# A gated dilated convolution: the first lines of x loaded in pieces of 112 and 15 partitions, and the zero halo written after the transpose

## The chip, the core and the metric

The kernel runs on one core of a Trainium2 chip. The metric is the device time of one execution in microseconds, the median of several. The profile is of one execution; its span runs from the first to the last instruction of the core and is about 2 us shorter than the time.

## The reference

```python
B, T, D, K = (2, 16000, 144, 15)          # x: (B, T, D), w: (K, D, 2D), w_o: (D, D), all bfloat16
dil = 2
pad = (K - 1) * dil                       # 28
xp = jnp.pad(x, ((0, 0), (pad, 0), (0, 0)))
h = jnp.einsum('btc,cd->btd', xp[:, pad:pad + T, :], w[0])
for i in range(1, K):
    off = pad - i * dil
    h = h + jnp.einsum('btc,cd->btd', xp[:, off:off + T, :], w[i])
f = h[..., :D].copy()
g = h[..., D:].copy()
z = jnp.tanh(f) * _sigmoid(g)
return z @ w_o
```

A causal convolution along time with 15 taps, two steps apart; tanh of one half of the channels times the sigmoid of the other; then a projection. In front of each of the two batches stand 28 lines of zeros, the halo.

## The kernel before

The 32000 lines of x are cut into 128 segments of L = 250 lines, one for each partition; partitions 0 to 63 are batch 0 and 64 to 127 batch 1 (SEG = 64). A partition needs the H = 28 lines ahead of its segment too. For all partitions but two these are the last lines of the segment before. For partitions 0 and 64, where a batch begins, they are zero.

The tile Xp holds the first 38 lines of each partition (28 of halo, 2 odd ones up to E0 = 30, and one group of 8, an "octet"). It is loaded in four pieces along time: lines 0 to 14, 14 to 22, 22 to 30 and 30 to 38. The text calls them x0, x1, x2 and x3. Weights come in four pieces of 3 or 4 taps, w3 first. Xr is the tile for the chunks of 16 lines that follow.

```python
LOADS = [("x", 0), ("w", 3), ("w", 2), ("x", 1), ("w", 1), ("x", 2), ("x", 3), ("r", 0), ("w", 0)]
pro_pieces = [(0, 14), (14, 22), (22, E0), (E0, EP)]
...
# x0, x1, x2: two loads of 63 partitions each (1..63 and 65..127)
for i, p0 in enumerate((0, SEG)):
    g.add("sp", ld_x(flat(Xp[p0 + 1:p0 + SEG, e0:e1, :]), p0 + 1, p0 + SEG, e0, e1), w=[("Xp", pi, i)], ...)
...
# partitions 0 and 64: the two real lines by a load, the 28 zero lines by four memsets on VectorE
for p0 in (0, SEG):
    g.add("act", ld_x(flat(Xp[p0:p0 + 1, H:E0, :]), p0, p0 + 1, H, E0), w=[("Xp", 2, 2 + p0)], ...)
for zi, (e0, e1) in enumerate(((0, 14), (14, H))):
    for p0 in (0, SEG):
        g.add("dve", lambda v, ...: v.memset(flat(Xp[p0:p0 + 1, e0:e1, :]), 0.0), w=[("XpZ", zi, p0)], dur=1.1)
```

Channels 0 to 127 of each line are transposed on TensorE, so that channels lie on partitions; the result is copied from PSUM into XA, one octet at a time, by VectorE for the first and ScalarE for the others. Channels 128 to 143 are copied by ScalarE into XBc, from where four lines at a time are transposed later into XB. A warm-up of 40 matmuls stands ahead of the first transposes in TensorE's order.

```python
warm(40)
...
for pi in range(4):
    for o in range(-4, 1):                   # octets -4 .. 0, those that begin in this piece
        ...
        g.add("pe", fns, r=xp_keys[pi] + ["ID"], alloc=[bk], ...)            # transposes (L575)
        eng = "dve" if o == -4 else "act"
        g.add(eng, ev, r=[bk], w=[("XA", aslot(o))], frees=[bk], ...)        # PSUM -> XA (L584)
    compact_pro(pi)                          # channels 128.. -> XBc, on ScalarE (L544, L562)
hk = ["XBc_h%d" % i for i in range(4)]
hk5 = hk + ["XBc_h4"]
for o, tiles, bb in ((-1, range(E0 - 4, E0), 7), (0, range(E0, E0 + 8), 6)):
    ...                                      # transposes of XBc (L594), copied to XB by ScalarE (L598)
```

The first ten output lines of each segment are computed directly, 15 taps each, from XA and the weights ("direct" matmuls); the scheduler uses them to fill TensorE's time until the main part runs. The main part forms differences of lines and sums of weights on VectorE (V, DU, DD, GX, GU, GV, GD; WC, WS, WT, WD) and needs fewer matmuls for each line. Its lines come from Xr, copied by ScalarE into STA (L637) and transposed by DMA.

Each operation is given to a small list scheduler in the kernel, with the keys that it reads (`r`) and writes (`w`) and an assumed duration; from these the order on each engine and the semaphore waits are worked out. All matmuls of the convolution have one source line, L725, and all main loads of x have L475.

Of the kernel before, what the change touches and what calls it, by code (L numbers as in the profile page):

```python
# [11 lines left out]
NP = 128  # L12
# [315 lines left out]
def _conv_wavenet_kernel(nc, x, w, w_o, out):  # L328
    B, T, D = x.shape
    K = w.shape[0]  # L330
    DIL = 2
    DA = 128
    DB = D - DA
    N2 = 2 * D
    total = B * T
    L = total // NP
    SEG = T // L
    H = DIL * (K - 1)
    assert (B, T, D, K) == (2, 16000, 144, 15) and L * NP == total and T % L == 0
    NT = L  # L340
    KD = NT % 8
    NOCT = NT // 8
    assert KD == 2
    E0 = H + KD
    NE_ALL = L + H
    MB = (NE_ALL + 2) // 4 + 1
# [30 lines left out]
    with contextlib.ExitStack() as st:  # L377
        def sb(name, shape, dt):
            return st.enter_context(nc.sbuf_tensor(name, shape, dt))

        Xp = sb("Xp", [NP, EP, D], BF16)
        Xr = sb("Xr", [NP, NX, XCH, D], BF16)
        XBc = sb("XBc", [NP, 8, MB, DB], BF16)
        STA = sb("STA", [NP, NST, 8, 128], BF16)
        STB = sb("STB", [NP, NST, 12, 128], BF16)
        XA = sb("XA", [NP, NA, 8, 128], BF16)
# [26 lines left out]
        x_t, w_t, wo_t, out_t = x.tensor, w.tensor, w_o.tensor, out.tensor  # L413

        g = _Graph()
# [25 lines left out]
        def aslot(o):  # L441
            return (o + 4) % NA
# [7 lines left out]
        def bslot(o):  # L450
            return (o + 1) % NB

        def oct_of(e):
            return (e - E0) // 8, (e - E0) % 8
# [9 lines left out]
        def win_b(e):  # L464
            c4, m4 = (e + 2) % 4, (e + 2) // 4
            return XBc[:, 4 + c4, MB - 1 - m4:MB - 1 - m4 + 8, :].rearrange("p m c -> p (m c)")
# [5 lines left out]
        def ld_x(tile_ap, p0, p1, e0, e1):  # L472
            def f(e):
                src = bass.AP(x_t, (p0 * L - H + e0) * D, [[L * D, p1 - p0], [1, (e1 - e0) * D]])
                return e.dma_start(tile_ap, src)  # L475
            return f

        def flat(ap):
            return ap.rearrange("p e d -> p (e d)")
# [4 lines left out]
        def ld_w(t0, t1):  # L484
            def f(e):
                src = bass.AP(w_t, t0 * D * N2, [[N2, DA], [D * N2, t1 - t0], [1, N2]])
                return e.dma_start(WA[:, t0:t1, :], src)  # L487
            return f
        wa_pieces = [(0, 4), (4, 8), (8, 12), (12, 15)]
        LOADS = [("x", 0), ("w", 3), ("w", 2), ("x", 1), ("w", 1), ("x", 2), ("x", 3), ("r", 0), ("w", 0)]  # L490
        pro_pieces = [(0, 14), (14, 22), (22, E0), (E0, EP)]
        def load_xchunk(ci):
            a, c = CH[ci]
            s = ci % NX
            return g.add("sp", ld_x(flat(Xr[:, s, 0:c - a, :]), 0, NP, E0 + a, E0 + c), w=[("Xr", s)], dur=0.5, dma="xr", nbytes=NP * (c - a) * D * 2)

        wa_ops = {}
        for what, pi in LOADS:
            if what == "w":
                t0, t1 = wa_pieces[pi]  # L500
                wa_ops[pi] = g.add("sp", ld_w(t0, t1), w=[("WA", pi)], dur=0.42, dma="wa", nbytes=(t1 - t0) * 128 * N2 * 2)
                continue
            if what == "r":
                load_xchunk(pi)
                continue
            e0, e1 = pro_pieces[pi]
            if e0 >= H:
                g.add("sp", ld_x(flat(Xp[:, e0:e1, :]), 0, NP, e0, e1), w=[("Xp", pi, 0), ("Xp", pi, 1)], dur=0.48, dma="xp", nbytes=NP * (e1 - e0) * D * 2)
                continue
            for i, p0 in enumerate((0, SEG)):  # L510
                g.add("sp", ld_x(flat(Xp[p0 + 1:p0 + SEG, e0:e1, :]), p0 + 1, p0 + SEG, e0, e1), w=[("Xp", pi, i)], dur=0.48, dma="xp", nbytes=63 * (e1 - e0) * D * 2)
        for p0 in (0, SEG):
            g.add("act", ld_x(flat(Xp[p0:p0 + 1, H:E0, :]), p0, p0 + 1, H, E0), w=[("Xp", 2, 2 + p0)], dur=0.5, dma="xp", nbytes=576)
        for zi, (e0, e1) in enumerate(((0, 14), (14, H))):
            for p0 in (0, SEG):
                g.add("dve", lambda v, p0=p0, e0=e0, e1=e1: v.memset(flat(Xp[p0:p0 + 1, e0:e1, :]), 0.0), w=[("XpZ", zi, p0)], dur=1.1)
        xpz = [[("XpZ", zi, p0) for p0 in (0, SEG)] for zi in range(2)]
        xp_keys = [[("Xp", 0, 0), ("Xp", 0, 1)] + xpz[0], [("Xp", 1, 0), ("Xp", 1, 1)] + xpz[1],
                   [("Xp", 2, 0), ("Xp", 2, 1), ("Xp", 2, 2), ("Xp", 2, 2 + SEG)] + xpz[1], [("Xp", 3, 0), ("Xp", 3, 1)]]
        wa_op = wa_ops[0]  # L520

        def ld_wb(par):
            n = 8 - par
# [25 lines left out]
        def warm(n):  # L549
            bk = _Bank(BANK_O)  # L550
            g.add("pe", [lambda t: t.matmul(PS[:, BANK_O * 512:BANK_O * 512 + 128], lhsT=ID[:], rhs=ONES[:], start=True, stop=True)] * n,
                  r=["ID", "ONES"], alloc=[bk], frees=[bk], dur=0.07 * n)
# [3 lines left out]
        def compact_pro(pi):  # L556
            e0, e1 = pro_pieces[pi]
            if pi == 0:
                def f2(a):
                    s = Xp[:, 0:2, DA:D]  # L560
                    dst = bass.AP(XBc[:].tensor, 6 * MB * DB + (MB - 1) * DB, [[8 * MB * DB, NP], [MB * DB, 2], [1, DB]])
                    return a.activation(dst, s, ACT.Copy)  # L562
                g.add("act", f2, r=xp_keys[0], w=["XBc_h0"], dur=0.25)
                e0 = 2
            cmp_op("act", Xp[:, e0:e1, DA:D], e0, e1, xp_keys[pi], "XBc_h%d" % (pi + 1), 0.35)
        for pi in range(4):
            e0, e1 = pro_pieces[pi]
            for o in range(-4, 1):
                es = [e for e in range(max(0, E0 + 8 * o), E0 + 8 * o + 8)]
                if not (e0 <= es[0] < e1):  # L570
                    continue
                b = 6 + o % 2
                fns = []
                for e in es:
                    fns.append((lambda e_, b_, i_: (lambda t: t.transpose(PSb[:, b_ * 1024 + 128 * i_:b_ * 1024 + 128 * i_ + 128], Xp[:, e_, 0:DA], ID[:])))(e, b, oct_of(e)[1]))  # L575
                bk = _Bank(b)
                g.add("pe", fns, r=xp_keys[pi] + ["ID"], alloc=[bk], dur=0.06 * len(es))
                i0 = oct_of(es[0])[1]
                eng = "dve" if o == -4 else "act"

                def ev(v, b_=b, i0_=i0, o_=o, eng_=eng):
                    dst = XA[:, aslot(o_), i0_:8, :].rearrange("p a b -> p (a b)")
                    src = PSb[:, b_ * 1024 + 128 * i0_:b_ * 1024 + 1024]
                    return v.activation(dst, src, ACT.Copy) if eng_ == "act" else v.tensor_copy(dst, src)  # L584
                g.add(eng, ev, r=[bk], w=[("XA", aslot(o))], frees=[bk], dur=0.92 if eng == "act" else 0.6)
            compact_pro(pi)
            warm(WARMS)
        hk = ["XBc_h%d" % i for i in range(4)]
        hk5 = hk + ["XBc_h4"]
        for o, tiles, bb in ((-1, range(E0 - 4, E0), 7), (0, range(E0, E0 + 8), 6)):  # L590
            fns = []
            for e in tiles:
                c0 = bb * 1024 + 128 * oct_of(e)[1]
                fns.append(lambda t, e_=e, c=c0: t.transpose(PSb[:, c:c + 128], win_b(e_), ID[:]))  # L594
            bk = _Bank(bb)
            g.add("pe", fns, r=hk5 + ["XBcz", "ID"], alloc=[bk], dur=0.06 * len(fns))
            i0 = oct_of(tiles[0])[1]
            xb_op = g.add("act", lambda v, o=o, i0=i0, bb=bb: v.activation(XB[:, bslot(o), i0:8, :].rearrange("p a b -> p (a b)"), PSb[:, bb * 1024 + 128 * i0:bb * 1024 + 1024], ACT.Copy),  # L598
                  r=[bk], w=[("XB", bslot(o))], frees=[bk], dur=0.5 if o < 0 else 0.92)
# [275 lines left out]
        def octs(u):  # L875
            m, r = units[u]
            return m, r, 2 * m + 1, 2 * m + 2
# [183 lines left out]
        if ("r", 0) not in LOADS:  # L1061
            load_xchunk(0).deps.add(wa_op)
# [75 lines left out]
        def fetch(o):  # L1138
            while nl[0] < len(CH) and CH[nl[0]][0] <= 8 * o:
                load_xchunk(nl[0]).deps.add(wa_op if nl[0] < 2 else xb2)  # L1140
                nl[0] += 1
# [47 lines left out]
        for t in range(-reach, NUN):  # L1189
# [3 lines left out]
            for name, off in pattern_of(t):  # L1193
# [20 lines left out]
                if name[0] == "D":  # L1214
                    done_d[u] = done_d.get(u, 0) + 1
                    m, r, o0, o1 = octs(u)
# [12 lines left out]
        m, r, o0, o1 = octs(NUN - 1)  # L1229
# [53 lines left out]
def bass_standalone__autoregressive_conv_wavenet__speech_kernel(  # L1283
    nc: bass.Bass,
    x: bass.AP,
    w: bass.AP,
    w_o: bass.AP,
    out: bass.AP,
):
    _conv_wavenet_kernel(nc, x, w, w_o, out)  # L1290
# [28 lines left out]
```

## Time and profile before

| what | value | where from |
|---|---|---|
| time | 325.68 us median of 3 (324.48, 325.68, 325.94) | times |
| span of the profiled execution | 322.6 us | page, first line |
| DVE memsets of the halo (L516) | 4, 898 ns each, from 1.11 to 5.50 us | timeline |
| Xp loads of x0, each half | 63 packets of 4032 B | packet records |
| Xp loads of x1 and x2, each half | 63 packets of 2304 B | packet records |
| granted TensorE clock | 1.000 | clock of the core |

How to read it: PE is TensorE, DVE VectorE, ACT ScalarE, POOL GpSimd and SP SyncE, which issues most of the loads. A line of a timeline has the start in us, the duration in us, the engine, the source line, the operation, what is written and read, the number of instructions put together and, in brackets, how long the engine sat idle ahead of it and what ended that. A line of the list of waits has who waited for whom, the total in us, how often, and the longest. In the chain that ended last a line has start, duration and what held the end at that time.

### The profile page before, as it was taken

How to read it: one execution, taken by the hardware profiler on the slowest of the kernel's cores; microseconds unless marked ns; L12 is line 12 of the kernel's file. 1: busy time of each engine (PE TensorE's matmuls, PEld its weight loads, DVE VectorE, ACT ScalarE, POOL GpSimd, SP SyncE). 2: the span in 40 equal slices, each digit the busy share in tenths (PEclk: the TensorE clock that was granted, in tenths of full speed). 3: DMA queues.
4: the chain of work that ended last, by engine and by line, in shares of the span. 5: the costliest groups of instructions: out<-in, count | busy, mean ns of one | idle time of the engine just before them, and what ended most of it. 6: DMA issues, size and time to landing. Idle time of an engine off the chain costs nothing.

```text
span 322.6 us, 6961 instructions
## 1 busy us (share of the span) xinstructions
PE 314.0 (97%) x2670; PEld 243.0 (75%) x2670; DVE 285.8 (89%) x610; ACT 269.4 (83%) x636; POOL 15.4 (5%) x26
## 2 busy tenths in 40 slices
PE   7899999999999999999999999999999999999994
PEld 6677777777777777777777777777777777777673
DVE  6699989899898989989898999989899998884773
ACT  3599689889798988979798897979889797778674
POOL 8005500000000000000000000000000000000000
PEclk9999999999999999999999999999999999999999
DMA  7799995967779297886959589793958477131653
GB/s 180 221 204 147 265 189 124 170 165 163 191 119 259 58 222 144 125 229 89 251 104 231 129 180 172 117 269 63 218 138 176 104 137 175 44 69 71 112 132 91
DMA packets 127780, 50.38 MB, mean 156 GB/s; under 512 B 119095, under 2 KB 121577, under 8 KB 127747
## 3 DMA queue, kind: packets, MB, share of 16 engines
q1 hardware_dynamic: 127231, 49.61, 74.2%
q0 software_dynamic: 512, 0.33, 0.5%
q8 instruction: 21, 0.34, 0.5%
q14 instruction: 12, 0.10, 0.1%
q10 hardware_dynamic: 4, 0.00, 0.0%
HBM read 11.81 MB, written 9.22 MB: 65 GB/s over the span
## 4 chain that ended last, share of the span: by engine, by line
PE 86%; DVE 4%; ACT 4%; DMA 3%; SPq 1%; issue 1%; ACTq 0%
PE PS L725 76%; PE PS L824 9%; DMA Xr<-in_x_dram 3%; SPq L475 1%; ACT STA L637 1%; ACT STB L657 1%; DVE V L677 1%; DVE Xp L1004 1%; DVE DD L677 1%; ACT XB L598 0%; DVE DU L677 0%; SPq L487 0%; PE PS L855 0%; DVE Z L754 0%; PE PS L782 0%
## 5 line engine op out<-in xcount | busy, mean ns | idle before, releaser
L1004 DVE TENSOR_TENSOR Xp<-PS,UX 128x576 f32<-128x576 f32 x90 | 62.8, 750 | 19.6 <-PE PS L725 19.3
L725 PE MATMUL PS<-WB,XB 128*128 128x288 bf16 x260 | 71.8, 286 | 0.1
L1016 DVE TENSOR_TENSOR PS<-PS,Xp 128x576 f32<-128x576 f32 x90 | 68.2, 757 | 2.1 <-ACT OS L832 1.0
L725 PE MATMUL PS<-WA,GD 128*128 128x288 bf16 x360 | 69.9, 286 | 0.0
L746 ACT ACTIVATE TS<-PS 128x288 f16<-128x288 f32 x125 | 51.6, 413 | 11.7 <-PE PS L725 10.7
L832 ACT ACTIVATE OS<-PS 128x432 bf16<-128x432 f32 (+1 forms) x88 | 42.3, 488 | 13.8 <-PE PS L824 12.8
L749 ACT ACTIVATE TS<-PS 128x288 f16<-128x288 f32 x125 | 51.4, 411 | 0.0
L657 ACT ACTIVATE STB<-XBc 128x768 bf16<-128x768 bf16 x60 | 50.7, 853 | 0.1
L883 ACT ACTIVATE PS<-PS 128x288 f32<-128x288 f32 x120 | 46.2, 407 | 3.6 <-PE PS L725 3.3
L952 ACT ACTIVATE UX<-PS 128x576 f32<-128x576 f32 x60 | 39.3, 655 | 10.3 <-PE PS L725 10.1
L725 PE MATMUL PS<-WS,GU 128*128 128x288 bf16 x210 | 44.3, 287 | 0.0
L824 PE MATMUL PS<-WOR,ZT 128*128 128x144 bf16 (+1 forms) x322 | 42.4, 253 | 0.0
L725 PEld LDWEIGHTS PS<-WA,GD 128*128 128x128 bf16 x360 | 34.6, 98 | 9.8 <-DVE PS L1016 0.9
L754 DVE TENSOR_TENSOR Z<-TS 128x288 bf16<-128x288 f16 x125 | 36.7, 299 | 4.6 <-ACT TS L749 4.3
L725 PE MATMUL PS<-WC,XB 128*128 128x288 bf16 x120 | 34.3, 286 | 0.0
L824 PEld LDWEIGHTS PS<-WOR,ZT 128*128 128x128 bf16 x322 | 27.9, 98 | 6.3 <-ACT OS L832 0.5
L725 PE MATMUL PS<-WD,DD 128*128 128x288 bf16 x180 | 31.9, 286 | 0.5 <-ACT PS L883 0.5
L725 PE MATMUL PS<-WA,DD 128*128 128x288 bf16 x180 | 30.6, 286 | 0.0
L725 PE MATMUL PS<-WC,V 128*128 128x288 bf16 x180 | 30.6, 286 | 0.0
L725 PEld LDWEIGHTS PS<-WB,XB 128*128 128x128 bf16 x260 | 25.4, 98 | 6.7 <-ACT XB L598 0.4
L725 PE MATMUL PS<-WT,DU 128*128 128x288 bf16 x120 | 24.5, 286 | 0.1
L677 DVE TENSOR_TENSOR V<-XA 128x1024 bf16<-128x1024 bf16 (+2 forms) x39 | 23.5, 607 | 0.9 <-ACT XA L584 0.9
(80 smaller groups left out, 464.3 us busy)
## 6 DMA issues: line engine op xcount, KB each, us to landing
Xr<-in_x_dram SPq DMA_DIRECT2D x15, 576.0 KB, 4.6
out_dram<-OS SPq DMA_DIRECT2D x30, 288.0 KB, 3.1
WA<-in_w_dram SPq DMA_DIRECT2D x3, 288.0 KB, 7.6
Xp<-in_x_dram SPq DMA_DIRECT2D x4, 141.8 KB
ZT<-Z SPq DMA_TRANSPOSE x32, 3.7
Xp<-in_x_dram SPq DMA_DIRECT2D x2, 248.1 KB
XA<-STA SPq DMA_TRANSPOSE x30, 3.4
XB<-STB SPq DMA_TRANSPOSE x30, 5.0
```

The lines of the kernel that those rows point to most:

```text
L657: return v.activation(STB[:, q, 6 * h:6 * h + 6, :], src, ACT.Copy)
L677: return g.add("dve", lambda v: v.tensor_tensor(dst, a, b, ALU.subtract), r=r, w=wk, dur=t_tt(n), prio=prio, soft=gate[:1])
L725: return lambda t: t.matmul(bank(bk.b), lhsT=lhs(), rhs=rhs(), start=start, stop=True, skip_group_check=True)
L746: return a.activation(TS[:, s, 0, :, :], both(bk, 0, D), ACT.Tanh)
L749: return a.activation(TS[:, s, 1, :, :], both(bk, D, D), ACT.Sigmoid)
L754: return v.tensor_tensor(dst, TS[:, s, 0, :, :], TS[:, s, 1, :, :], ALU.mult)
L824: return t.matmul(PS[:, c0:c0 + n * D], lhsT=ZT[:, zt, blk, :], rhs=WOR[:, wi:wi + n, :].rearrange("p a b -> p (a b)"), start=first, stop= ...
L832: return e.tensor_copy(dst, src) if eng == "dve" else e.activation(dst, src, ACT.Copy)
L883: g.add("act", lambda e: e.activation(bank(bk.b + 1), bank(bk.b), ACT.Copy), w=[bk], dur=t_act(N2), prio=0)
L952: g.add("act", lambda e: e.activation(UX[:, k, u % NU, :, :], both(X, 0, N2), ACT.Copy), r=[X], w=[("UX", k, u % NU)], frees=[X], dur=t_ac ...
L1004: g.add("dve", lambda v, k=k, wi=wi, vb=vb, us=us: v.tensor_tensor(wslot(wi), both(vb, 0, N2), UX[:, k, us, :, :], ALU.add), r=[vb, ("UX", ...
L1016: return v.tensor_tensor(both(d, 0, N2), src, wslot(wi), ALU.add)
```

## The change

Each of the pieces x0, x1 and x2 is loaded for partitions 1 to 112 by one DMA and for partitions 113 to 127 by another, whatever batch they belong to. Partition 64 so gets the last lines of batch 0 in its halo, and partition 0 gets the first lines of x as a filler, by one more DMA of 8064 bytes, so that nothing unset is read. The zeros are set later: in XA, where the two partitions have become two columns of each transposed line, by four memsets on VectorE, and in XBc by two memsets on GpSimd, each on one partition. These two also clear the two real lines in XBc that share the range, and one more GpSimd copy puts them back. The memsets of Xp are dropped. The purpose is a number of partitions that is a multiple of 16 in the large loads, and no clearing ahead of the transposes. The order of loads, the transposes, the copies and the main part are as before.

```diff
+        n16 = ((NP - 1) // 16) * 16
...
-            for i, p0 in enumerate((0, SEG)):
-                g.add("sp", ld_x(flat(Xp[p0 + 1:p0 + SEG, e0:e1, :]), p0 + 1, p0 + SEG, e0, e1), w=[("Xp", pi, i)], dur=0.48, dma="xp", nbytes=63 * (e1 - e0) * D * 2)
-        for p0 in (0, SEG):
-            g.add("act", ld_x(flat(Xp[p0:p0 + 1, H:E0, :]), p0, p0 + 1, H, E0), w=[("Xp", 2, 2 + p0)], dur=0.5, dma="xp", nbytes=576)
-        for zi, (e0, e1) in enumerate(((0, 14), (14, H))):
-            for p0 in (0, SEG):
-                g.add("dve", lambda v, p0=p0, e0=e0, e1=e1: v.memset(flat(Xp[p0:p0 + 1, e0:e1, :]), 0.0), w=[("XpZ", zi, p0)], dur=1.1)
...
+            g.add("sp", ld_x(flat(Xp[1:1 + n16, e0:e1, :]), 1, 1 + n16, e0, e1), w=[("Xp", pi, 0)], dur=0.48, dma="xp", nbytes=n16 * (e1 - e0) * D * 2)
+            g.add("sp", ld_x(flat(Xp[1 + n16:NP, e0:e1, :]), 1 + n16, NP, e0, e1), w=[("Xp", pi, 1)], dur=0.48, dma="xp", nbytes=15 * (e1 - e0) * D * 2)
+        g.add("act", lambda e: e.dma_start(flat(Xp[0:1, 0:H, :]), bass.AP(x_t, 0, [[L * D, 1], [1, H * D]])), w=[("Xp", 0, 2)], dur=0.5, dma="xp", nbytes=8064)
+        g.add("act", lambda e: e.dma_start(flat(Xp[0:1, H:E0, :]), bass.AP(x_t, 0, [[L * D, 1], [1, KD * D]])), w=[("Xp", 2, 2)], dur=0.5, dma="xp", nbytes=576)
...
+        for o in range(-4, 0):
+            i0 = 2 if o == -4 else 0
+            i1 = 6 if o == -1 else 8
+            def zc(v, o_=o, i0_=i0, i1_=i1):
+                dst = XA[:, aslot(o_), i0_:i1_, :].rearrange("p s (b q) -> p s b q", q=SEG)[:, :, :, 0]
+                return v.memset(dst, 0.0)
+            g.add("dve", zc, w=[("XA", aslot(o))], dur=0.08)
...
+        for b in range(B):
+            def zf(p, b_=b):
+                return p.memset(XBc[b_ * SEG:b_ * SEG + 1, 4:8, MB - H // 4 - 1:MB, :], 0.0)
+            g.add("pool", zf, r=hk, w=hk + ["XBcz"], dur=0.35)
...
+        def fix(p):
+            s = Xp[:, H:E0, DA:D]
+            dst = bass.AP(XBc[:].tensor, 6 * MB * DB + (MB - 1 - H // 4) * DB, [[8 * MB * DB, NP], [MB * DB, 2], [1, DB]])
+            return p.tensor_copy(dst, s)
+        g.add("pool", fix, r=xp_keys[2], w=hk, dur=0.3)
```

More of the change, by code (lines that the diff above doesn't have):

```diff
@@ L509, in _conv_wavenet_kernel @@
                 continue
-            for i, p0 in enumerate((0, SEG)):
-                g.add("sp", ld_x(flat(Xp[p0 + 1:p0 + SEG, e0:e1, :]), p0 + 1, p0 + SEG, e0, e1), w=[("Xp", pi, i)], dur=0.48, dma="xp", nbytes=63 * (e1 - e0) * D * 2)
-        for p0 in (0, SEG):
-            g.add("act", ld_x(flat(Xp[p0:p0 + 1, H:E0, :]), p0, p0 + 1, H, E0), w=[("Xp", 2, 2 + p0)], dur=0.5, dma="xp", nbytes=576)
-        for zi, (e0, e1) in enumerate(((0, 14), (14, H))):
-            for p0 in (0, SEG):
-                g.add("dve", lambda v, p0=p0, e0=e0, e1=e1: v.memset(flat(Xp[p0:p0 + 1, e0:e1, :]), 0.0), w=[("XpZ", zi, p0)], dur=1.1)
[L517 to L520, printed above, removed]
+            g.add("sp", ld_x(flat(Xp[1:1 + n16, e0:e1, :]), 1, 1 + n16, e0, e1), w=[("Xp", pi, 0)], dur=0.48, dma="xp", nbytes=n16 * (e1 - e0) * D * 2)
+            g.add("sp", ld_x(flat(Xp[1 + n16:NP, e0:e1, :]), 1 + n16, NP, e0, e1), w=[("Xp", pi, 1)], dur=0.48, dma="xp", nbytes=15 * (e1 - e0) * D * 2)
+        g.add("act", lambda e: e.dma_start(flat(Xp[0:1, 0:H, :]), bass.AP(x_t, 0, [[L * D, 1], [1, H * D]])), w=[("Xp", 0, 2)], dur=0.5, dma="xp", nbytes=8064)
+        g.add("act", lambda e: e.dma_start(flat(Xp[0:1, H:E0, :]), bass.AP(x_t, 0, [[L * D, 1], [1, KD * D]])), w=[("Xp", 2, 2)], dur=0.5, dma="xp", nbytes=576)
+        wa_op = wa_ops[LOADS[-1][1]] if LOADS[-1][0] == "w" else wa_ops[0]
+        xp_keys = [[("Xp", 0, 0), ("Xp", 0, 1), ("Xp", 0, 2)], [("Xp", 1, 0), ("Xp", 1, 1), ("Xp", 0, 2)],
+                   [("Xp", 2, 0), ("Xp", 2, 1), ("Xp", 0, 2), ("Xp", 2, 2)], [("Xp", 3, 0)]]
         def ld_wb(par):
```

## The prediction

> **What bounds the kernel now.** I read the page's busy shares first, then who waits for whom, the chain that ended last, the start of the timeline, and the DMA packets. On the page, TensorE (PE) is busy nearly all the time:
>
> ```profile
> PE 314.0 (97%) x2670; PEld 243.0 (75%) x2670; DVE 285.8 (89%) x610; ACT 269.4 (83%) x636; POOL 15.4 (5%) x26
> ```
>
> The waits of PE over the whole span are five:
>
> ```profile
> PE PS L551 <- POOL ID L529: 1.7, 1, 1.7
> PE PS L575 <- DMA Xp<-in_x_dram: 1.6, 3, 0.8
> PE PS L725 <- ACT PS L883: 0.5, 1, 0.5
> PE PS L782 <- ACT Xr L777: 0.4, 1, 0.4
> PE PS L725 <- DVE XA L584: 0.2, 1, 0.2
> ```
>
> The change touches the second (the transposes wait for the lines of x) and the fifth. The other three are the wait before the warm-up and two in the last 45 us. Where the second falls is seen in PE's own timeline of the stretch 5 to 15 us:
>
> ```profile
> 4.73 1.14 PE L551 MATMUL PS<-ONES,ID 128*128 128x128 bf16 x11
> 6.33 0.95 PE L575 MATMUL PS<-ID,Xp 128*128 128x128 bf16 x14 [0.46 <-DMA Xp<-in_x_dram]
> 7.50 2.19 PE L725 MATMUL PS<-WA,XA 128*128 128x288 bf16 x15 [0.21 <-DVE XA L584]
> 10.05 0.62 PE L575 MATMUL PS<-ID,Xp 128*128 128x128 bf16 x8 [0.37 <-DMA Xp<-in_x_dram]
> 10.51 1.51 PE L725 MATMUL PS<-WA,XA 128*128 128x288 bf16 x11
> 12.84 0.61 PE L575 MATMUL PS<-ID,Xp 128*128 128x128 bf16 x8 [0.82 <-DMA Xp<-in_x_dram]
> 13.28 1.14 PE L725 MATMUL PS<-WA,XA 128*128 128x288 bf16 x8
> 14.26 0.61 PE L575 MATMUL PS<-ID,Xp 128*128 128x128 bf16 x8
> ```
>
> The warm-up ends at 4.73 + 1.14 = 5.87. From there to 12.84 PE waits 0.46 + 0.37 + 0.82 = 1.65 us for Xp. After 12.84 the list above has nothing until the end phase, so time gained before about 13 us can reach the end, if the other engines keep up. Whether they do is read from the chain that ended last, in order of time:
>
> ```profile
> 4.69 1.13 SPq L475
> 5.86 8.97 DMA Xr<-in_x_dram
> 14.85 1.06 ACT STA L637
> 15.91 0.91 ACT XA L584
> ...
> 39.61 5.43 PE PS L725 x42
> ```
>
> It runs through the first main chunk of x (Xr), landed at 14.83, then without a gap over ScalarE (ACT) and VectorE (DVE) to 39.6 us, where PE takes over. So the gain is the smaller of two shifts: what PE saves before 13 us, and how much sooner Xr lands.
>
> The trace's packet records explain the loads. The first 63-line load of Xp, whose rows are 4032-byte packets, ends in nine 4-byte completion packets (3.49 to 3.72 us), Xr in nine late ones (14.09 to 14.31 us). From 4 to 11 us the core moves some 270 GB/s (mean of half-microsecond bins of packet starts); from about 11.5 us, with Xr not yet finished, the bins fall to 130 to 280 GB/s. Packet durations while loaded: 4032 B 156 ns, 2304 B about 120, 4608 B about 182, 576 B (weights) 31.
>
> **What the Trainium skill says.** "DMA: Bandwidth & Descriptors", section "Why a DMA increments its semaphore by 16 and not by 1": a copy runs on the largest number of engines up to 16 that divides the slowest dimension of both sides, the lowest-numbered ones, and each engine used posts one completion. For 63 lines that is 9, for 112 it is 16, for 15 it is 15, and for all 127 lines in one piece it would be 1, which explains two pieces. The nine completions agree for 63; no trace yet shows 112 or 15. The same page's "Rules for kernel authors" says that two loads of disjoint partition halves both spray over all 16 engines; for 63-line halves this trace differs, with nine. "SBUF — State Buffer", section "SBUF: two separate sides", says that DVE and GpSimd (POOL) share a port pair under an exclusive lock; no contention can be seen here before, because POOL is idle from 7.50 us until it issues the WOR loads at 28.15.
>
> **What is removed.** Engines 0 to 8 carry 14 rows of each of the three Xp pieces, engines 9 to 15 none. Up to Xr, one of the nine carries: x0 14 x 0.156 = 2.18, w3 24 x 0.031 = 0.74, w2 32 x 0.031 = 0.99, x1 14 x 0.120 = 1.68, w1 0.99, x2 1.68, x3 8 x 0.120 = 0.96, Xr 8 x 0.182 = 1.46; sum 10.68 us. After the change each carries 7 + 1 rows per piece. It saves 6 x 0.156 = 0.94 us by x0, another 6 x 0.120 = 0.72 by x1, another 0.72 by x2: 2.38 us by Xr. With all 16 busy throughout, the common rate may bind instead. Xp, the three weight pieces and Xr are 1.40 + 0.81 + 0.59 = 2.80 MB; at 270 GB/s that is 10.4 us, from about 2.4 us (the first packets took 0.47 to 0.59 us each) to 12.8, against a last packet at 14.31. So Xr lands 1.5 us sooner by the rate and 2.4 by the rows; I take 1.5, and 1.1 if the rate is a tenth lower.
>
> The Xp pieces were usable at 6.31, 10.03 and 12.77. By the rows they come at about 5.4, 8.4 and 10.4. The four DVE clears of a halo line (898 ns each, 1.11 to 5.50 us) go too; they ended before x0 was usable, with DVE otherwise idle, so they are worth nothing.
>
> **What it means for PE.** x0 at 5.4 is before the warm-up's end at 5.87, so only 0.46 is gained there. The second transposes would be reached at 9.69 - 0.46 = 9.23 and x1 is there at 8.4: 0.37 gained. The third at 12.02 - 0.83 = 11.19, x2 at 10.4: 0.82 gained. Sum 1.65 us.
>
> **What is added.** Four DVE memsets of at most 128x16 elements, each between the copy of a transposed octet into XA and the matmuls on it. The 128x32 uint32 memset of SCR took 85 ns, so 0.09 each, plus a handoff of some 0.05 (DVE's copy ends at 7.44, PE starts at 7.50), plus the rest of a weight sum that DVE may be in (L608, 300 to 450 ns). For the octet that DVE copies itself I count 0.14; for the next, 0.25, as PE's weight loads already wait for it (8.40). For the last two PE should have other matmuls to do. Sum about 0.4 us. Two POOL memsets on one partition of 512 elements: Z's memset took 3930 ns for 4608, so about 0.44 each; with the copy of 128x32 (an estimate of 0.2, from the 117 ns of POOL's memset of that size) 1.1 us after the third piece's copy into XBc. That was done at 13.08 and XBc is first used at 15.14, so it fits. The junk line for partition 0 is 8064 B, two more rows for one engine, about 0.3 us on x0, covered by the warm-up.
>
> Net: 1.65 - 0.4 = 1.25 us on PE, against 1.1 to 2.4 on the chain through Xr. Expected gain about 1.3 us: 325.7 - 1.3 = 324.4 us.
>
> **The rivals.** (a) The clears become the wait: DVE works in order, and a clear queued behind a sum whose weights are not there holds PE. For it: DVE sat 1.60 us before a WC sum for weights at 11.05. Against it: weights also come sooner. It would eat 0.5 to 1 us more: 325.2 to 325.7. (b) The common rate binds harder than 270 GB/s and Xr hardly moves: ACT, gapless from 14.85 to 24, and DVE behind it then keep their times, and PE runs out of early matmuls and waits: 325.4. For it: bins of 165 to 215 GB/s at 5 to 6 and 8.5 us with all engines at work. Against it: bins of 300 to 349 elsewhere. (c) Everything shifts by the full amount, the clears hidden: 1.65 to 2.2 us, 323.5 to 324.0. (d) The kernel orders its instructions by an internal plan; other operations may reorder DVE and ACT work later, by some tenths either way.
>
> **Range and chances.** Mechanism: 0.2 to 2.1 us of gain. The three times before lie 1.46 us apart, so a median may be off by 0.6. Together 322.8 to 325.8. Two per cent is 6.5 us, more than all of PE's waits (4.4 us); losing that much would need a wait in the steady part, which the change doesn't touch.
>
> **What would show it.** Right: sixteen completions for the 112-line loads; transposes at 5.9 us with no wait on Xp at the second and third group; Xr landing at 12.5 to 13.7; the same 64-matmul groups of PE starting 1 to 1.5 us sooner. Wrong: Xr landing after 14.3; waits of PE on DVE XA or on the clears above 0.5 us; new waits of PE between 14 and 45 us; POOL's copy holding the transposes of XBc.

## The result, and the profile after

The kernel after takes 322.49 us (median of 6, 321.80 to 323.22) against 324.81 us (median of 6, 324.00 to 325.94) before. The ratio is 0.9925 with a 95% interval of 0.9898 to 0.9952: 2.4 us less, 1.6 to 3.3 by the interval. The unchanged kernel timed again beside other runs gave 0.9934 (0.9912 to 0.9956). The forecast was 324.4 us in a range of 322.8 to 325.8, so the kernel is faster than that range.

Two things make the difference of 1.9 us. The median of three from which I started (325.68) was high: before came to 324.81 with six times, and to 324.39, 324.70 and 324.78 in the later comparisons. That is 0.9 us, where the prediction allowed for 0.6. The gain itself was forecast as 1.3 us, and it is 2.3 us in span (322.6 to 320.3).

Busy times on the page of the kernel after; TensorE has the same 2670 matmuls as before:

```profile
PE 313.1 (98%) x2670; PEld 243.4 (76%) x2670; DVE 282.5 (88%) x610; ACT 269.6 (84%) x636; POOL 16.9 (5%) x29
```

Its list of all waits of PE:

```profile
PE PS L548 <- POOL ID L526: 1.7, 1, 1.7
PE PS L740 <- DVE XA L590: 0.6, 1, 0.6
PE PS L740 <- ACT PS L898: 0.5, 1, 0.5
PE PS L797 <- ACT Xr L792: 0.4, 1, 0.4
```

The wait for Xp has gone altogether. The clears (L590) stand where VectorE's copy into XA stood. That wait was 0.2 us before, when it was for the copy alone. PE's own timeline from 5 to 15 us:

```profile
4.75 1.28 PE L548 MATMUL PS<-ONES,ID 128*128 128x128 bf16 x11
5.87 0.94 PE L572 MATMUL PS<-ID,Xp 128*128 128x128 bf16 x14
7.38 1.29 PE L740 MATMUL PS<-WA,XA 128*128 128x288 bf16 x9 [0.57 <-DVE XA L590]
8.51 0.61 PE L572 MATMUL PS<-ID,Xp 128*128 128x128 bf16 x8
8.96 1.76 PE L740 MATMUL PS<-WA,XA 128*128 128x288 bf16 x13
10.55 0.61 PE L572 MATMUL PS<-ID,Xp 128*128 128x128 bf16 x8
10.99 1.14 PE L740 MATMUL PS<-WA,XA 128*128 128x288 bf16 x8
11.97 0.61 PE L572 MATMUL PS<-ID,Xp 128*128 128x128 bf16 x8
```

The second and third groups of transposes start without a wait, 1.54 and 2.29 us sooner than before. Only nine matmuls stand ahead of the second group where there were fifteen: the kernel's plan put the others later.

The chain that ended last, from the third transposes on:

```profile
10.71 0.46 PE PS L572 x8
11.19 1.02 ACT XA L581
12.22 0.20 ACT XBc L541
12.42 0.95 ACT STA L652
13.36 0.91 ACT XA L581
...
37.36 6.17 PE PS L740 x48
```

It no longer runs through the landing of Xr but through TensorE and ScalarE to the same copy of Xr into STA. That copy starts at 12.31 us (before 14.85; in the chain it counts from 12.42, when the operation ahead of it ended). Far behind, in the main part, each group of 64 matmuls starts 2.24 us sooner. The second of these groups in each chain, kernel before and then kernel after:

```profile
74.83 7.89 PE PS L725 x64
```
```profile
72.59 7.89 PE PS L740 x64
```

The start of this group is the mark of each run below ("the group"), because what follows it is nearly the same in all of them.

The packet records show the loads. The 4032-byte packets of Xp end at 4.65 us (before 5.38), the last of the first Xr chunk at 11.71 (before 14.32). The core moves 341 to 406 GB/s in the half-microsecond bins from 10 to 12 us, where it moved 130 to 349 before. Up to 10.27 us, when the last piece of Xp is in, 157 completion packets of 4 bytes are recorded on SyncE's queue. That is what 16 and 15 for each of x0, x1 and x2 and 16 for each of three weight pieces and x3 add up to, so the sixteen completions that the prediction named as a sign of being right are there.

### The profile page after: what moved, and what is told of

Same layout as the page of the kernel before. It is cut to its first block, busy times and chain, and to the rows that moved or that the text cites. A ratio compares the mean times of both kernels' runs of the same rounds, so it can differ in the third digit from the quotient of the medians.

```text
span 320.3 us, 6963 instructions
## 1 busy us (share of the span) xinstructions
PE 313.1 (98%) x2670; PEld 243.4 (76%) x2670; DVE 282.5 (88%) x610; ACT 269.6 (84%) x636; POOL 16.9 (5%) x29
## 4 chain that ended last, share of the span: by engine, by line
PE 89%; ACT 5%; DVE 2%; DMA 2%; issue 1%; POOL 0%; ACTq 0%; POOLq 0%
PE PS L740 77%; PE PS L839 9%; DMA XA<-STA 2%; PE PS L548 1%; ACT STA L652 1%; ACT STB L672 1%; ACT XA L581 1%; DVE Xp L1019 0%; ACT XB L613 0%; PE PS L572 0%; DVE DD L692 0%; ACT TS L764 0%; PE PS L870 0%; PE PS L797 0%; ACT OS L847 0%
## 5 line engine op out<-in xcount | busy, mean ns | idle before, releaser
L847 ACT ACTIVATE OS<-PS 128x432 bf16<-128x432 f32 (+1 forms) x88 | 42.3, 488 | 13.7 <-PE PS L839 12.8
L967 ACT ACTIVATE UX<-PS 128x576 f32<-128x576 f32 x60 | 39.2, 654 | 10.4 <-PE PS L740 10.1
L740 PEld LDWEIGHTS PS<-WS,GU 128*128 128x128 bf16 x210 | 18.5, 98 | 7.5 <-ACT PS L898 0.3
```

What stands on the lines that cost most here:

```text
L740: return lambda t: t.matmul(bank(bk.b), lhsT=lhs(), rhs=rhs(), start=start, stop=True, skip_group_check=True)
L847: return e.tensor_copy(dst, src) if eng == "dve" else e.activation(dst, src, ACT.Copy)
L967: g.add("act", lambda e: e.activation(UX[:, k, u % NU, :, :], both(X, 0, N2), ACT.Copy), r=[X], w=[("UX", k, u % NU)], frees=[X], dur=t_ac ...
```

## The experiments

Two kinds are to be told apart. In the runs marked "same order" the order of instructions on TensorE, VectorE and ScalarE is that of the kernel after to the last row, and only loads (or the number of warm-up matmuls) differ. In the others the kernel's own plan also reordered its work. In most of these that mattered more than what they were meant to change. In one, the run without the clears of XA, the order of TensorE, VectorE and ScalarE is, but for the memsets, exactly that of the kernel before.

**Loads of 63 and 64 lines, same order.** The sizes in the plan were left as they were and only the split was moved.

```diff
-            g.add("sp", ld_x(flat(Xp[1:1 + n16, e0:e1, :]), 1, 1 + n16, e0, e1), ...)
-            g.add("sp", ld_x(flat(Xp[1 + n16:NP, e0:e1, :]), 1 + n16, NP, e0, e1), ...)
+            g.add("sp", ld_x(flat(Xp[1:1 + 63, e0:e1, :]), 1, 1 + 63, e0, e1), ...)
+            g.add("sp", ld_x(flat(Xp[1 + 63:NP, e0:e1, :]), 1 + 63, NP, e0, e1), ...)
```

> Kernel after, the order of instructions on every engine unchanged, but each piece loaded as 63 and 64 lines (9 and 16 engines: 7 + 4 = 11 rows of each piece on engines 0 to 8, where the kernel after has 8). Theory (rows on the busiest engine set the time): 3 x 0.396 = 1.2 us more; Xr lands at 13.3 to 13.7 us (after 12.31), the first regular group of 64 matmuls starts at 73.5 to 74.0 (after 72.59), ratio to before 0.995 to 0.998. Rival (the clearing or the new order of operations gave the gain): group at 72.6, ratio 0.9925.

**49 and 78 lines, same order.** The same edit with 49 for 63.

> The same with 49 and 78 lines (7 and 13 engines: 7 + 6 = 13 rows on engines 0 to 6, one fewer than in the kernel before). Theory: 5 x 0.396 = 2.0 us more than after; Xr lands at 14.0 to 14.5, group of 64 at 74.3 to 75.0, ratio 0.998 to 1.001. Rival: group at 72.6, ratio 0.9925.

Measured: with 63 and 64 lines the copy of Xr starts at 14.29 us and the group at 74.97, ratio 0.9995 (0.9980 to 1.0009); with 49 and 78 lines 14.78 and 74.98, ratio 0.9999 (0.9985 to 1.0013). ScalarE's first copy of Xr, from the timelines of the kernel after, of 63 and 64, and of 49 and 78:

```profile
12.31 1.05 ACT L652 ACTIVATE STA<-Xr 128x1024 bf16<-128x1024 bf16 x1
```
```profile
14.29 1.06 ACT L652 ACTIVATE STA<-Xr 128x1024 bf16<-128x1024 bf16 x1
```
```profile
14.78 1.06 ACT L652 ACTIVATE STA<-Xr 128x1024 bf16<-128x1024 bf16 x1
```

The group in the chains of 63 and 64, and of 49 and 78:

```profile
74.97 7.89 PE PS L740 x64
```
```profile
74.98 7.89 PE PS L740 x64
```

And in the 49 and 78 run PE's two waits for Xp are back:

```profile
10.05 0.62 PE L572 MATMUL PS<-ID,Xp 128*128 128x128 bf16 x8 [0.58 <-DMA Xp<-in_x_dram]
12.81 0.61 PE L572 MATMUL PS<-ID,Xp 128*128 128x128 bf16 x8 [0.55 <-DMA Xp<-in_x_dram]
```

So with the clears and the order of the kernel after, an uneven split alone gives the whole gain back. The clears, the new order and the loss of the memsets on Xp bring nothing by themselves. The run without the clears, below, is the other half: it has the loads of 112 and 15 lines with the order of the kernel before, and it keeps the gain. The count of rows is only half right. For 11 rows it gives 1.2 us and the copy came 2.0 us later; for 13 rows 2.0 and 2.5. In the 63 and 64 run packets slow down in places: 576-byte ones take 71 and 72 ns instead of 31 between 4.5 and 5.5 us, and the 4608-byte ones that start between 11.0 and 11.5 us take 495 ns on average instead of 182. Why is open.

**113 and 14 lines, same order.** One line moved from one piece to the other.

> Kernel after, order of instructions unchanged, each piece loaded as 113 and 14 lines in place of 112 and 15. 113 is prime, so one engine should carry all 113 rows. Theory: 105 rows more on the busiest engine, 105 x 0.396 = 42 us; ScalarE begins its first copy of Xr at 50 to 58 us, time 360 to 372 us. Rival (sizes and piece boundaries matter, not divisibility): the same as after, 322.5 us.

Measured once: 359.45 us, and ScalarE's first copy of Xr starts at 47.84 us, both just under what was expected. PE's timeline has

```profile
21.57 1.68 PE L572 MATMUL PS<-ID,Xp 128*128 128x128 bf16 x14 [16.00 <-DMA Xp<-in_x_dram]
```

and the packet records show 4032-byte packets one after the other, every 155 ns or so, from 2.2 to 21.0 us: one engine, some 26 GB/s. A shift of one line costs 37 us, so what counts is divisibility and not the size of the pieces. This is the rule given in the prediction from the Trainium skill, "DMA: Bandwidth & Descriptors", section "Why a DMA increments its semaphore by 16 and not by 1", and this run agrees with it.

**Xr issued behind the last weights, same order.** After the plan was made, two issues of SyncE were exchanged.

```diff
         _ms = g.schedule()
+        sp = g.order["sp"]
+        ir = [i for i, op in enumerate(sp) if op.dma == "xr"][0]
+        iw = [i for i, op in enumerate(sp) if op.dma == "wa"][-1]
+        sp[ir], sp[iw] = sp[iw], sp[ir]
```

> Kernel after with only the issues of the first Xr chunk and of the last weight piece exchanged; Xp comes as in the kernel after, Xr about 32 x 0.031 = 1.0 us later (13.2 to 13.5). If the chain through Xr and ScalarE binds beside TensorE's own work: group of 64 at 73.2 to 73.7, ratio 0.994 to 0.997. If only the waits for Xp and TensorE's own work bind: group at 72.6, ratio 0.9925.

Measured: ratio 0.9975 (0.9957 to 0.9992), group at 74.07, which is 0.4 us beyond the range of the first theory. In ScalarE's timeline

```profile
13.60 1.06 ACT L652 ACTIVATE STA<-Xr 128x1024 bf16<-128x1024 bf16 x1 [0.82 <-DMA Xr<-in_x_dram]
```

The copy is 1.29 us later and the group 1.48 us than in the kernel after. A part of that is not the change: in this execution PE's slow start, told of in the last section, lasted until 6.56 us instead of 5.79. The kernel after, run again (below), had the same slow start, until 6.55 us. Against it the copy is 0.93 us later and the group 1.23. Counted from start to start beyond the usual spacing, PE loses 1.09 us before 15 us in both, but 1.81 instead of 0.65 between 15 and 50. So the landing of Xr does set the end once it is late, beside PE's own work.

**34 warm-up matmuls instead of 40.** The order is the same.

```diff
-        warm(40)
+        warm(34)
```

> Kernel after with 34 warm-up matmuls in place of 40; x0 is usable at 5.42 us, the warm-up ended at 5.87. TensorE can start its transposes 0.4 us sooner. If TensorE alone binds: group of 64 at 72.2, ratio 0.991. If the chain from Xr over ScalarE binds too: the 0.4 us comes back as waits between 15 and 50 us and the group stays at 72.5 to 72.6.

Measured: ratio 0.9933 (0.9914 to 0.9952), group at 72.91, no gain. PE's first line behind the warm-up is

```profile
5.28 1.54 PE L572 MATMUL PS<-ID,Xp 128*128 128x128 bf16 x14
```

The transposes start 0.59 us sooner, but eleven of the thirteen steps between them take 107 ns instead of 56, as in the warm-up, up to 6.45 us in this execution. The first matmuls on XA start 0.23 us sooner (7.15), and that is lost again by the second transposes. These start at 8.51 as in the kernel after. The two theories are not told apart by this: the start was lost ahead of the place where they differ.

**Without the clears of XA, in the order of the kernel before.** The four memsets are left out, so the halo columns hold other lines of x and the first lines of each batch come out otherwise.

```diff
-            g.add("dve", zc, w=[("XA", aslot(o))], dur=0.08)
```

> Kernel after without the four VectorE clears of XA, so the halo columns hold other lines of x (part of the computation left out). Theory: the clears cost 0.1 to 0.4 us; group of 64 at 72.2 to 72.5 (after 72.59). Rival (the clears are a large wait on the path): 71.6 or less. If they are hidden altogether: 72.6.

Measured: ratio 0.9945 (0.9928 to 0.9961), group at 72.56. Without the clears the plan went back to the order of the kernel before, with fifteen matmuls ahead of the second transposes:

```profile
6.73 2.19 PE L739 MATMUL PS<-WA,XA 128*128 128x288 bf16 x15 [0.20 <-DVE XA L581]
```

So the gain is there with the old order as well, and only the loads and the dropped memsets of Xp are left to give it. The runs with 63 and 64, and 49 and 78 lines drop these memsets too and have no gain, so it is the loads. PE loses 0.54 us before 15 us instead of 0.74, and 1.23 instead of 0.78 between 25 and 50. Its first matmuls on XA start 0.65 us sooner than in the kernel after, 0.29 of that because the warm-up ended sooner in this execution. ScalarE's copy of Xr starts at 12.32, as with the clears. So the clears and the order that they bring cost 0.2 us on the spot and nothing at the end. That an earlier PE alone gains nothing fits this, but the order differs too, so it is not shown by itself.

**The clears alone, with loads of 63 lines.** Here the order changed. Partition 64 was filled by one more load of 8640 bytes from ScalarE.

```diff
+            for i, p0 in enumerate((0, SEG)):
+                g.add("sp", ld_x(flat(Xp[p0 + 1:p0 + SEG, e0:e1, :]), p0 + 1, p0 + SEG, e0, e1), w=[("Xp", pi, i)], ...)
+        g.add("act", lambda e: e.dma_start(flat(Xp[SEG:SEG + 1, 0:E0, :]), ...), w=[("Xp", 0, 3)], ...)
```

> The new clearing (four VectorE memsets on XA, three GpSimd operations on XBc) with the loads of 63 lines as before. Theory (nine engines against sixteen is the whole gain): Xp is waited for as before, Xr lands near 14.8 us, the first regular group of 64 matmuls starts at 74.8 to 75.2 us (before 74.83, after 72.59), ratio to before 1.000 to 1.002. Rival (the clearing, or the order of operations that it brings, gave the gain): group at 72.6 to 73.5, ratio 0.993 to 0.996.

Measured: ratio 1.0149 (1.0111 to 1.0187), group at 78.42, outside both expectations. VectorE's timeline shows what happened:

```profile
8.28 0.45 DVE L624 TENSOR_TENSOR WS<-WA 128x576 bf16<-128x576 bf16 x1
8.64 0.30 DVE L624 TENSOR_TENSOR WC<-WC 128x288 bf16<-128x288 bf16 x1
8.86 0.55 DVE L582 COPY XA<-PS 128x768 bf16<-128x768 bf16 x1
```

The copy into XA, which starts at 6.40 in the kernel after, was placed behind six weight sums, and PE's matmuls on it behind the second transposes, which wait for x1. PE stood from about 7.6 to 10.1 us and again until 11.65:

```profile
10.08 0.61 PE L573 MATMUL PS<-ID,Xp 128*128 128x128 bf16 x8 [2.30 <-DMA Xp<-in_x_dram]
11.65 3.29 PE L741 MATMUL PS<-WA,XA 128*128 128x288 bf16 x15 [0.97 <-DVE XA L591]
```

Its matmuls from 11.9 to 14.3 us then start 240 ns apart instead of 122. The run says nothing of the clears' own cost. The runs with 63 and 64, and 49 and 78 lines replace it.

**The kernel before with each half cut into 48 and 15 lines.** Even loads, zeros set in Xp as before.

```diff
-                g.add("sp", ld_x(flat(Xp[p0 + 1:p0 + SEG, e0:e1, :]), ...), w=[("Xp", pi, i)], ...)
+                for j, (q0, q1) in enumerate(((1, 49), (49, SEG))):
+                    g.add("sp", ld_x(flat(Xp[p0 + q0:p0 + q1, e0:e1, :]), ...), w=[("Xq", pi, i, j)], ...)
```

> Kernel before with each 63-line load cut into 48 and 15 lines, all issued by SyncE; zeros set in Xp as before, no clears later. Theory: eight rows for each engine, as in the kernel after, but six more issues of some 0.4 us; Xr lands at 12.3 to 13.0, group of 64 at 72.2 to 73.2, ratio 0.991 to 0.995. Rival (the clearing or its order gave the gain): as before, 74.8, ratio 1.000.

Measured: ratio 0.9988 (0.9973 to 1.0004); copy of Xr at 13.89, group at 73.80, between the two expectations, while the ratio fits the rival. The execution in the trace was the fastest of twenty (323.16 us, median 323.81), so its group looks better than the ratio. PE's loss before 15 us fell to 1.10 us (before 2.68), but between 25 and 50 us it rose to 2.13 (before 0.95). The two largest new waits there are PE's weight loads for ScalarE:

```profile
PEld PS L727 <- ACT UX L954: 0.9, 1, 0.9
PEld PS L727 <- ACT PS L912: 0.8, 1, 0.8
```

ScalarE's early operations stand in another order in this kernel: it copies XB ahead of the second STA and of the STB copies (STB is for the channels in XBc what STA is for the others). That this order is what cost it was not tried by itself.

**The same with the 15-line pieces issued by ScalarE.** The edit is the one above with "act" for the second piece.

> As the run with 48 and 15 lines, but the 15-line pieces are issued by ScalarE, which is idle then. Theory: Xr lands at 12.1 to 12.6; no clear stands before the first matmuls on XA, so TensorE's idle start-to-start time before 15 us is 0.3 to 0.5 us (after 0.74); group of 64 at 72.0 to 72.6, ratio 0.990 to 0.993. Rival: as before, 74.8.

Measured: ratio 1.0178 (1.0145 to 1.0210), group at 80.67. This kernel computes something else than the reference, and why is open, so it is read only for where PE waited. Again the copy into XA stands behind six weight sums (it starts at 9.03), PE idles 2.41 us ahead of 9.64 and its matmuls then start 240 ns apart.

**Xr ahead of x3, and ahead of x2.** Two attempts at a faster kernel, by the order of loads.

```diff
-        LOADS = [..., ("w", 1), ("x", 2), ("x", 3), ("r", 0), ("w", 0)]
+        LOADS = [..., ("w", 1), ("x", 2), ("r", 0), ("x", 3), ("w", 0)]     # ahead of x3
+        LOADS = [..., ("w", 1), ("r", 0), ("x", 2), ("x", 3), ("w", 0)]     # ahead of x2
```

> Kernel after with the first Xr chunk loaded ahead of x3. In the runs so far the first regular group of 64 matmuls starts 60.2 us (59.9 to 60.7) after ScalarE begins its first copy of Xr. If that start is what binds: copy at 11.3 to 12.2, group at 71.5 to 72.4, ratio 0.989 to 0.992. If ScalarE's whole early work binds (the copies of x3 only move behind): 72.3 to 73.0, ratio 0.992 to 0.995.

> Kernel after with the first Xr chunk loaded ahead of x2 and x3. If the start of the first copy of Xr binds: copy at 10.0 to 10.7, group at 70.3 to 71.0, ratio 0.985 to 0.988. If ScalarE's whole early work or the direct matmuls on late x2 bind: group at 72.3 to 73.5, ratio 0.992 to 0.997.

Measured: 0.9988 (0.9974 to 1.0003) and 1.0004 (0.9985 to 1.0024). The copy of Xr started at 12.91 and 10.35 us, the groups at 75.32 and 74.55; neither group lies in a range I had given. In the second the copy came 2 us sooner than in the kernel after and the group 2 us later. An early copy alone is worth nothing when the order behind it changes. No version tried was faster than the kernel after.

**The kernel after again.**

> The kernel after itself, unchanged, on the chip of these runs: ratio to before 0.991 to 0.995, first regular group of 64 matmuls at 72.3 to 72.9 us.

Measured: 0.9934 (0.9912 to 0.9956), copy of Xr at 12.67, group at 72.84.

Put together, the runs with the order of the kernel after (start of the copy of Xr, start of the group, difference, in us):

| run | copy of Xr | group | difference |
|---|---|---|---|
| after | 12.31 | 72.59 | 60.28 |
| after again | 12.67 | 72.84 | 60.17 |
| 34 warm-up matmuls | 12.39 | 72.91 | 60.52 |
| Xr behind w0 | 13.60 | 74.07 | 60.47 |
| 63 and 64 lines | 14.29 | 74.97 | 60.68 |
| 49 and 78 lines | 14.78 | 74.98 | 60.20 |
| 113 and 14 lines | 47.84 | 109.50 | 61.66 |

With one order of instructions the main part starts 60.2 to 60.7 us behind ScalarE's first copy of Xr (61.7 in the extreme run). With other orders it can be near (59.98 in the kernel before, 60.24 without the clears, 59.91 with 48 and 15 lines) or far off: 62.41 and 64.20 with Xr moved up, 63.39 and 67.39 in the two runs with the late copy into XA.

## Why the prediction was wrong

The mechanism was right. The loads are the gain, nine engines against sixteen. What failed is the sizes in the sum, above all PE's waits for Xp and the landing of Xr, and the base was 0.9 us too high.

*"I take 1.5"*, the landing of Xr. I had 2.38 us by the rows of the busiest engine and 1.5 by a common rate of 270 GB/s, and chose the rate. ScalarE's copy of Xr starts 2.54 us sooner, and the last packet landed at 11.71 instead of 12.8. Rival (b), a rate that binds, did not happen. The 270 GB/s taken from the kernel before was no ceiling: from 4 to 10 us it moved 258 GB/s and the kernel after 293, and from 10 to 12 us, where mostly large packets remained, the kernel after moved 371. The rows were the better estimate of the two here, though the 63 and 64 run shows that they can miss by 0.8 us. The prediction took the usual duration of a packet (156 ns for 4032 B, 120 for 2304 B); the means up to 16 us in that trace are 244 and 131, so a sum of rows comes out too small where packets slow down.

*"Sum 1.65 us"*, PE's waits for Xp. The list counts a wait from the modelled end of the matmul before it, and matmuls overlap. Counted from start to start beyond the usual spacing (56 ns for 128 columns, 122 for 288), PE lost 0.63 + 0.53 + 0.98 = 2.14 us there, half a microsecond more. All of PE's losses before 15 us were 2.68 us, and are now 0.74; those from 15 to 50 us, of which the list shows none and the prediction counted none, fell from 1.17 to 0.78. Together 2.33 us, which is the gain in span. This is the step that failed most: 1.25 us net was forecast on PE, where 1.94 came before 15 us and 0.39 after it.

*"Sum about 0.4 us"*, the clears. On PE's path the loss between transposes and first matmuls went from 0.54 us (0.37 and 0.17) to 0.74, so 0.2. In the run without them, which has another order too, this doesn't reach the end. They are quick, 68 and 72 ns (0.09 us forecast), but the first one stands behind two weight sums in VectorE's order, as rival (a) had it:

```profile
6.40 0.56 DVE L581 COPY XA<-PS 128x768 bf16<-128x768 bf16 x1 [5.42 <-PE PS L572]
6.88 0.30 DVE L623 TENSOR_TENSOR WC<-WA 128x288 bf16<-128x288 bf16 x1
7.11 0.29 DVE L623 TENSOR_TENSOR WS<-WA 128x288 bf16<-128x288 bf16 x1
7.17 0.07 DVE L590 MEMSET XA<- 128x12 bf16 x1
```

*"The smaller of two shifts"* fits what was measured. PE's came out at 2.33 us and that of Xr at 2.54, so neither cut off much of the other. The late-Xr run shows the chain through Xr binding; that PE alone gains nothing is not shown without a change of order beside it.

What was right: x0 was usable at 5.42 us (5.4 forecast), x1 at about 8.05 (8.4), x2 by 10.16 (10.4). The warm-up kept the transposes until 5.8 us. POOL's three operations took 1.09 and 0.45 us and ended at 12.13, ahead of the transposes of XBc at 14.87. Rival (c), everything shifted by the full amount, is what happened, and by 2.3 us a little beyond its 1.65 to 2.2. Rival (a) shows as a wait of 0.57 us on the clears, above the 0.5 us that the prediction named as a sign of being wrong, and yet the gain came. Rival (d), the plan's order, was called some tenths; in the two worst of the six runs where the order changed the group came 6 and 8 us later than in the kernel after, and in five of the six the change under study can't be read by itself.

Open are: why packets slow down in places, why the kernel with ScalarE issues computes something else, and which operation's place in ScalarE's order costs the late waits.

## What to carry to other kernels

Count the rows that one DMA engine gets, not the bytes of a load: cut a load of n partitions so that most of it has a multiple of 16 of them, and never leave a prime number above 16 in one piece. Fill what mustn't be loaded with anything finite and zero it later where that is cheap. When a change is to be judged in a kernel that plans its own order, hold the order fixed and change only the transfer, or the order will answer in its place; and measure TensorE's waits from start to start.

## What the runs showed of the hardware that was not expected

One line more in a load, 113 for 112, took the load of x0 from 4.65 us to 21.0 us, with one 4032-byte packet every 155 ns.

TensorE fell to half its rate after short idle times. In the run with ScalarE issues, PE stood 2.6 us from start to start (7.01 to 9.64 us); from 9.9 to 13.3 us its 288-column matmuls started 240 ns apart and its transposes 107, and from then on 122 for the former again. The run with the clears alone did the same after 2.5 and 1.1 us of idle time. The Trainium skill, "TensorE: Matmul & The Clock Gate", section "What's actually happening", gives about 3.4 us for an idle window, free-running; here less than that in one stretch was enough, and the slow time was 3.4 us.

The slow start at the beginning ended at 5.48 us in the trace of the kernel before, at 5.79 in that of the kernel after, and at 6.55 in that of the same kernel again. In the last the second transposes start at 8.86 instead of 8.51 us and the group is 0.25 us later. So a quarter of a microsecond between two traces may be this alone.

GpSimd's copy of 128x32 elements into XBc took 209 to 212 ns in the four runs in which VectorE did nothing meanwhile, and 322 to 690 ns in the seven in which it started while VectorE worked on a sum or difference (TENSOR_TENSOR). There it ended about 0.07 us after that operation. From the kernel after, and from 63 and 64 lines:

```profile
11.38 0.69 DVE L692 TENSOR_TENSOR DD<-V 128x1024 bf16<-128x1024 bf16 x1
11.68 0.45 POOL L603 COPY XBc<-Xp 128x32 bf16<-128x32 bf16 x1
```
```profile
13.75 0.21 POOL L603 COPY XBc<-Xp 128x32 bf16<-128x32 bf16 x1
```

This fits the lock that the prediction names, though no run tests it by itself. In the kernel after the copy took 0.45 us, where the prediction had estimated 0.2.
